# A recurrent attention block and its expert layer: the whole work order replaced by another

## The chip, the cores and the metric

The kernel runs on one core of a Trainium2 chip. The metric is device time in microseconds (us) of one execution; lower is better. The core has a matrix engine (PE in the profile, with its weight loads as PEld), three engines for elementwise work (DVE, ACT, POOL) and SP, which here only issues transfers. Each engine takes its instructions strictly in the order in which the program lists them; between engines only semaphores hold things together. So a list that says what comes after what on each engine decides when everything runs.

## The reference, cut to what matters

```python
for t in range(S):
    ...
    cur = np.einsum('bhd,bhe->bhde', u[None] * kt, vt)
    y[:, :, t] = np.einsum('bhd,bhde->bhe', rt, state + cur)
    state = w[None, :, :, None] * state + np.einsum('bhd,bhe->bhde', kt, vt)
...
pooled = x.mean(axis=1)
logits = pooled @ w_gate
e_idx = np.argmax(logits, axis=1)
...
    h = np.maximum(x[mask] @ w1[e], 0.0)
    out[mask] = gate_w[mask, None, None] * (h @ w2[e])
```

Batch is 4, heads 8, 768 steps, head width 48; x is the attention's output, (4, 768, 384), w1 is (8, 384, 1024), w2 (8, 1024, 384). A linear attention with a decaying state runs over four sequences of 768 steps; then each whole sequence is sent through one expert of eight, chosen from its mean.

## The kernel before, in words

Each sequence (batch b = 0 to 3) is cut into three blocks of 256 steps, so there are twelve blocks n = 0 to 11 with b = n / 3. The program is a set of small functions `do_X`, and a string of tokens, `ORDER`, which says in which order they are called. A token reads `what.arguments/engine@banks`: `E.5.1/V` calls `do_E` for block 5, half 1, on DVE; A is ACT, P is POOL; the digits behind @ are the PSUM banks (0 to 6) that its output takes. Tiles wait for each other by their data and by the reuse of a buffer or a bank; nothing else holds an engine. The scheduler does not move anything: an engine's queue is the string with the other engines' tokens taken out.

What the tokens do, along the path of a block:

- `L` loads k, r or v of a block (SP issues, L120); `cg` loads the gate's matrix (L263). `K` and `R` scale k and r by decay factors (POOL, L294; for block 0 in halves, `q`, `K.0`, `R.0`, L286). `V` casts v (tile vb).
- `T.n.0`, `T.n.1` turn scaled k and r on PE (tile tp, L325; from block 5 on L338). `E.n.0`, `E.n.1` copy the turned tiles out of PSUM (tile tw; L363 on DVE, L365 on ACT).
- `A` multiplies k with r on PE (tile at, L439), `G` masks the result on DVE (tile gt, L449): four per block, always DVE.
- `P`, `U`, `v`, `J` make the term of the current step: product on DVE or POOL, sum on PE (tile u, L399), times v (tile vt), and added on PE (L425). `t` copies a u tile out.
- `S` adds to the state on PE (L477, L468), `Z` decays it (DVE, L487), `s` copies it out (tile st), `y` multiplies r with it and `Y` the masked product with v, both on PE (tile y, L500).
- `N` casts the output out of PSUM (tile xn; L214 on DVE, L210 on ACT), `X` turns it on PE (tile xp, L538), `x` copies it to the expert's input xt; `p` and `g` sum it up.
- `l` is the gate's product on PE (tile lgp, L582, six matmuls), `m` takes the largest entry on DVE, `i` reads its number on POOL, `a` and `b` then load the chosen expert's first and second matrix (POOL issues, L627, L638). The transfer of the first matrix of batch 0 is split in two quarters, `a.0.q` and `a.0.0`, and a half, `a.0.1`.
- `M.b.f.s` is one group of the expert's first product (three matmuls into tile hp, L648; 64 tokens), `H` its ReLU (DVE or ACT, tile ht), `O.b.s.h` one group of the second (four matmuls into op, L683; 48 tokens), `o` the scaling by the gate, `B` the store (SP).
- `W.i.m` issues m matmuls of zeros into an otherwise unused bank (tile wp, L219); nothing reads them.

PE runs everything in one queue, so the groups `M` and `O` of one batch stand between the blocks of the next ones.

One thing ties loads to the expert's transfers: with `HOLD = (7, 8)` the loads of block 7 wait until the transfer `a.0.q` has landed, those of block 8 until the first `b` of a second half has (lines 267 to 276).

Of the kernel before, what the change touches and what calls it, by code (L numbers as in the profile page):

```python
# [24 lines left out]
v.0/P U.1@4 T.2.1@5 L.k.4 G.1.1.0/V Y.0@6 G.1.0.0/V y.1.0@1 y.1.1@0 s.2.0/A S.2.0 v.1/V Y.1 J.0 E.2.1/A
A.2.0@24 N.0.1/A N.0.0/A P.2/X K.3/P G.2.0.1/V G.2.0.0/V J.1 N.1.0/A N.1.1/A R.3/P L.r.4 L.v.4 A.2.1@53
G.2.1.0/V X.0@6 G.2.1.1/V V.3/A U.2@4 s.2.1/A T.3.0@1 p.0/V T.3.1@2 E.3.1/A X.1@0 E.3.0/V v.2/V p.1/V P.3/X
K.4/P y.2.1@5 S.3.0 s.3.1/A y.2.0@3 Y.2 J.2 N.2.0/A A.3.1@14 S.3.1 T.4.0@2 R.4/P x.1/A N.2.1/V Z.4/V G.3.1.0/V
X.2@3 E.4.0/A L.r.5 cg p.2/V g.0/V y.3.1@5 T.4.1@0 l.0@1 V.4/P G.3.1.1/V s.4.0/A m.0/V A.3.0@24 x.2/A x.0/A
E.4.1/A L.k.5 G.3.0.0/V G.3.0.1/V S.4.0 s.4.1/A W.2.4@1 U.3@3 v.3/V W.24.2@2 Y.3@6 e.0/A R.5/P L.r.6 A.4.0@14  # L30
A.4.1@23 P.4/X i.0/P S.4.1 a.0.q/P L.v.5 J.3 G.4.0.1/V G.4.1.0/V G.4.1.1/V G.4.0.0/V N.3.1/A N.3.0/A W.37.4@0
L.k.6 y.4.0@4 L.v.6 X.3@5 V.5/A U.4@0 K.5/P T.5.0@62 y.4.1@3 a.0.0/P T.5.1 Z.5/V p.3/A x.3/A Y.4 M.0.2.1@1
w.0/V E.5.0/V L.k.7 L.r.7 E.5.1/A s.5.0/A M.0.3.1@5 H.0.3.1/A H.0.2.1/A M.0.2.0@6 v.4/V H.0.2.0/V L.v.7 J.4
A.5.1@20 S.5.0 A.5.0@51 G.5.1.0/V a.0.1/P G.5.0.0/V M.0.0.1@6 K.6/P R.6/P P.5/P b.0.1/P N.4.1/A N.4.0/A
# [723 lines left out]
```

## Time and profile before

| | before |
|---|---|
| median of 3 runs | 129.71 us (129.59 to 130.69) |
| the profiled execution's own time | 129.35 us |
| its span, first to last instruction | 127.7 us |
| granted TensorE clock, mean | 0.999 of full speed |
| PE busy | 120.0 us (94%) |
| DVE, ACT, POOL busy | 84.7, 78.1, 78.0 us (66, 61, 61%) |
| moved by DMA | 25.5 MB |

The span leaves out what lies ahead of the first and behind the last instruction (1.6 us here). Busy shares are means over the span; the three elementwise engines do most of their work in the first 90 us, so a share read for a stretch says more than one of the whole. PE's matmuls overlap one another by their tails, so the duration of one (326 ns for a group's matmul of 384 columns) is longer than its share of PE's time (0.16 us, from a long row of them).

### The profile page before, as it was taken

What the parts mean: (1) busy time and instruction counts of PE and PEld (TensorE: products, weight loads), DVE (VectorE), ACT (ScalarE), POOL (GpSimd) and SP (SyncE); (2) the same over time, 40 slices, a digit from 0 to 9 for tenths busy, and PEclk for the clock granted to TensorE, in tenths of its full rate; (3) what the DMA queues carried; (4) which work ended last, traced back from release to release, by engine and by line L of the source; (5) the groups of instructions that cost most, each with busy time, mean ns of one, the idle gap of its engine ahead of it and who ended that gap; (6) DMA issues with size and microseconds to landing.
All of it is one profiled execution on the core that took longest, in us unless ns stands there. A gap on an engine that the chain in (4) does not pass through costs nothing.

```text
span 127.7 us, 4933 instructions
## 1 busy us (share of the span) xinstructions
PE 120.0 (94%) x2103; PEld 82.1 (64%) x2107; DVE 84.7 (66%) x192; ACT 78.1 (61%) x192; POOL 78.0 (61%) x72
## 2 busy tenths in 40 slices
...
GB/s 28 324 320 325 322 234 314 189 243 270 129 139 276 224 161 232 277 258 236 229 270 280 273 224 90 62 185 197 64 0 0 9 174 202 240 400 211 0 257 115
DMA packets 47768, 25.50 MB, mean 200 GB/s; under 512 B 38401, under 2 KB 46338, under 8 KB 47746
## 3 DMA queue, kind: packets, MB, share of 16 engines
...
## 4 chain that ended last, share of the span: by engine, by line
PE 91%; ACT 2%; DVE 2%; issue 2%; ACTq 0%
PE hp L648 25%; PE op L683 24%; PE y L500 8%; PE at L439 5%; PE wp L219 5%; PE tp L325 4%; PE tp L338 3%; PE xp L538 3%; PE s L468 3%; PE s L477 2%; PE lgp L582 2%; PE y L425 2%; PE u L399 2%; PE lnb L226 1%; PE op L673 1%
## 5 line engine op out<-in xcount | busy, mean ns | idle before, releaser
L648 PE MATMUL hp<-xt,w 128*128 128x384 bf16 x192 | 36.3, 326 | 0.0
L683 PE MATMUL op<-w,ht 128*128 128x384 bf16 x184 | 33.7, 326 | 0.0
L449 DVE TENSOR_TENSOR gt<-at,mask 128x512 bf16<-128x512 f32 x48 | 31.0, 683 | 3.8 <-PE at L439 3.5
L663 DVE TENSOR_SCALAR ht<-hp 128x384 bf16<-128x384 f32 x30 | 16.0, 552 | 13.3 <-PE hp L648 13.3
L683 PEld LDWEIGHTS <-ht 128*128 128x128 bf16 x184 | 17.4, 99 | 10.8 <-issue 0.2
L648 PEld LDWEIGHTS <-w 128*128 128x128 bf16 x192 | 17.4, 98 | 10.3 <-issue 0.3
L294 POOL TENSOR_TENSOR kp<-k,dk 128x768 bf16<-128x768 f32 x11 | 20.0, 1818 | 2.7 <-DMA k<-in_k_dram 2.1
L661 ACT ACTIVATE ht<-hp 128x384 bf16<-128x384 f32 x34 | 15.5, 501 | 9.4 <-PE hp L648 9.4
L294 POOL TENSOR_TENSOR rp<-r,dr 128x768 bf16<-128x768 f32 x11 | 20.0, 1814 | 1.6 <-DMA r<-in_r_dram 1.5
L704 ACT ACTIVATE ob<-op,gw 128x384 f32<-128x384 f32 (+1 forms) x17 | 9.5, 576 | 13.1 <-PE op L683 11.0
L627 POOL DMA_DIRECT2D w<-in_moe_w_dram x9 | 7.2, 797 | 15.7 <-issue 10.4
L365 ACT COPY tw<-tp 128x1024 bf16<-128x1024 bf16 x12 | 12.2, 1016 | 5.2 <-PE tp L338 4.6
L389 POOL TENSOR_TENSOR prod<-tw 128x1024 bf16<-128x1024 bf16 x6 | 12.7, 2121 | 1.8 <-DVE tw L363 1.8
L210 ACT CAST xn<-y 128x384 bf16<-128x384 f32 x22 | 9.7, 486 | 5.6 <-PE y L425 5.6
L706 DVE TENSOR_SCALAR ob<-op,gw 128x384 f32<-128x384 f32 (+1 forms) x8 | 4.6, 590 | 11.4 <-PE op L683 8.0
L495 ACT CAST st<-s 64x192 bf16<-64x192 f32 x32 | 10.1, 314 | 3.5 <-PE s L477 2.2
L219 PE MATMUL wp<-zeros 128*128 128x512 bf16 x30 | 9.0, 413 | 1.5 <-DVE zeros L135 1.4
L439 PE MATMUL at<-tw 64*64 64x128 bf16 x384 | 9.7, 219 | 0.4 <-DVE tw L363 0.2
L559 ACT ACTIVATE xt<-xp 128x256 bf16<-128x256 bf16 x21 | 7.8, 391 | 3.1 <-PE xp L538 3.1
L210 ACT CAST vb<-v 128x768 bf16<-128x768 f32 x10 | 8.4, 840 | 1.5 <-DMA v<-in_v_dram 1.5
L363 DVE COPY tw<-tp 128x512 uint32<-128x512 uint32 x12 | 8.1, 687 | 1.7 <-PE tp L338 0.8
L416 DVE TENSOR_TENSOR vt<-vb,u 128x768 bf16<-128x768 bf16 x8 | 7.6, 947 | 1.6 <-PE u L399 1.6
...
## 6 DMA issues: line engine op xcount, KB each, us to landing
w<-in_moe_w_dram POOLq DMA_DIRECT2D x15, 384.0 KB, 6.5
k<-in_k_dram SPq DMA_DIRECT2D x12, 384.0 KB, 5.2
r<-in_r_dram SPq DMA_DIRECT2D x12, 384.0 KB, 5.4
v<-in_v_dram SPq DMA_DIRECT2D x12, 384.0 KB, 5.9
out_dram<-ob SPq DMA_DIRECT2D x11, 384.0 KB, 6.9
w<-in_moe_w_dram POOLq DMA_DIRECT2D x2, 192.0 KB, 4.6
...
out_dram<-ob SPq DMA_DIRECT2D x1, 192.0 KB, 2.2
```

Source lines behind the costliest of these rows:

```text
L210: nc.scalar.copy(out, in_)
L219: nc.tensor.matmul(out=wp, lhsT=zeros[:, 0:128], rhs=zeros, start=True, stop=True)
L294: e.tensor_mul(dst[n % NR].rearrange("p (g a) d -> p a g d", a=2)[:, :, :, 0:D], *(t.rearrange("p (a q) j d -> p a (q j) d", a=2) for t in ...
L365: nc.scalar.copy(out, in_)
L389: e.tensor_mul(prod.rearrange("x g c p -> x c g p"), tk, tw[:, :, 1].rearrange("x c q j p -> x c (q j) p"))
L439: nc.tensor.matmul(out=at[a][64 * c : 64 * c + 64, 128 * q : 128 * q + 128], lhsT=tw[rows, c, 0, q, j, :], rhs=tw[rows, c, 1, q].rearrange ...
L449: nc.vector.tensor_mul(gts[n][:, j, a], ats[n, j][a].rearrange("x (q s) -> x q s", q=NQ), mask[:, j].rearrange("x j p -> x (j p)").unsquee ...
L500: nc.tensor.matmul(out=out, lhsT=lhsT, rhs=rhs, start=(n, c) not in begun, stop=False, skip_group_check=True)
L648: nc.tensor.matmul(out=hp[:, 0:SB], lhsT=wts[b][1][i][:, ct, 128 * f : 128 * f + 128], rhs=xts[b][:, ct, SB * sb : SB * sb + SB], start=(c ...
L661: nc.scalar.activation(out=o, in_=hp[:, 0:SB], func=ACT.Relu)
L663: nc.vector.tensor_scalar_max(o, hp[:, 0:SB], 0.0)
L683: nc.tensor.matmul(out=op[:, 0:DM], lhsT=hts[b, half][:, f, 128 * si : 128 * si + 128], rhs=wts[b][2][half][:, f, :], start=(half == 0 and ...
```

## The change

Only the string `ORDER` is replaced; every function, every buffer and every number of buffers stays. Both strings have 657 tokens and give PE the same 4168 rows of weight loads and matmuls. Apart from the labels of the filling matmuls and two small copies (`t.0` and `t.7` become `t.1` and `t.9`), the tokens are the same; they stand in another order, 72 have another engine, and nearly all PE tiles another bank.

```diff
-W.99.4@0 L.k.0 L.r.0 L.v.0 L.k.1 L.r.1 L.v.1 L.k.2 L.r.2 L.v.2 c.ln/A cB@0 c.dk.0/A c.dk.1/A W.33.2@1 W.15.2@2
...
+W.99.4@0 c.ln/A cB@0 c.dk.0/A c.dk.1/A c.dr.0/A c.dr.1/A L.k.0 q.k/P L.r.0 L.v.0 V.0/A L.k.1 W.37.2@1 W.2.4@2
...
```

The filling matmuls `W` number 34 in both; 14 stood ahead of the first `T` and 12 do now, and 10 stand behind `l.0` in both. On PE the same set of tokens stands ahead of the first `M` in both strings (fillers aside), in another sequence.

The first place is DVE's queue from its first copy out of PSUM on, that is blocks 0 and 1 (the digit behind a tile's letters is the block; for tp, gt and at further digits are halves). Before:

```order
L363 COPY tw0_221<-tp0_1_212 128x512
L363 COPY tw0_221<-tp0_0_227 128x512
L386 TENSOR_TENSOR prod0_251<-tp0_1_212,tw0_221 128x8x64 x2
L449 TENSOR_TENSOR gt0_290<-at0_01_255,mask_131 128x512
L449 TENSOR_TENSOR gt0_290<-at0_00_254,mask_131 128x512
L449 TENSOR_TENSOR gt0_290<-at0_10_272,mask_131 128x512
L487 TENSOR_TENSOR s0_237<-s0_237,wcT_168 128x384
L449 TENSOR_TENSOR gt0_290<-at0_11_273,mask_131 128x512
L363 COPY tw1_340<-tp1_1_342 128x512
L386 TENSOR_TENSOR prod1_375<-tp1_1_342,tw1_340 128x8x64 x2
```

DVE's queue at the same place, now:

```order
L363 COPY tw0_212<-tp0_1_214 128x512
L386 TENSOR_TENSOR prod0_240<-tp0_1_214,tw0_212 128x8x64 x2
L449 TENSOR_TENSOR gt0_286<-at0_11_244,mask_131 128x512
L449 TENSOR_TENSOR gt0_286<-at0_10_243,mask_131 128x512
L449 TENSOR_TENSOR gt0_286<-at0_00_261,mask_131 128x512
L487 TENSOR_TENSOR s0_223<-s0_223,wcT_168 128x384
L449 TENSOR_TENSOR gt0_286<-at0_01_262,mask_131 128x512
L416 TENSOR_TENSOR vt0_384<-vb0_182,u0_340 128x8x2x48
L386 TENSOR_TENSOR prod1_416<-tp1_1_312,tw1_337 128x8x64 x2
L449 TENSOR_TENSOR gt1_432<-at1_00_355,mask_131 128x512
```

Two of the three copies L363 have left the queue (`E.0.0` and `E.1.1`, now ACT's); the product with v of block 0 (L416) has come from POOL, which has that of block 1 instead. Up to the last `G` of block 4 one cast `N` goes (block 2) and one comes (block 3), one copy `p` goes and one copy `t` comes, and the rest of DVE's list is the same set.

The second place is DVE's queue behind the last `G` of block 5, with batch 0's `H` between the blocks. Before:

```order
L449 TENSOR_TENSOR gt5_1240<-at5_11_1189,mask_131 128x512
L663 TENSOR_SCALAR ht00_1172<-hp0_0_1_1245 128x384
L663 TENSOR_SCALAR ht00_1172<-hp0_1_0_1291 128x384
L363 COPY xt1_1117<-xp4_1261 128x2x3x64
L363 COPY tw6_1345<-tp6_0_1301 128x512
L416 TENSOR_TENSOR vt5_1371<-vb5_1062,u5_1347 128x8x2x48
L663 TENSOR_SCALAR ht10_1449<-hp0_6_0_1373 128x384
L214 CAST xn05_1455<-y5_0_1295 128x384
L449 TENSOR_TENSOR gt6_1467<-at6_10_1429,mask_131 128x512
```

The same place now:

```order
L449 TENSOR_TENSOR gt5_1282<-at5_00_1243,mask_131 128x512
L497 TENSOR_TENSOR st10_151<-s2_1308,bmask_155 128x384
L663 TENSOR_SCALAR ht10_1293<-hp0_6_1_1352 128x384
L363 COPY tw6_1407<-tp6_1_1318 128x512
L214 CAST xn05_1453<-y5_0_1357 128x384
L214 CAST xn15_1455<-y5_1_1367 128x384
L449 TENSOR_TENSOR gt6_1459<-at6_01_1416,mask_131 128x512
L363 COPY tw7_1496<-tp7_0_1462 128x512
L487 TENSOR_TENSOR s2_1308<-s2_1308,wcT_168 128x384
L363 COPY tw7_1496<-tp7_1_1463 128x512
```

Both casts of block 5 and both copies of block 7 are DVE's now. On PE, `Y.6`, which needs the four `G` of block 6, has moved up: behind the first `M` stood sixteen `M` and seven `O` ahead of it, now sixteen `M` and two `O`.

The third place is SP's queue, the loads of blocks 3 to 5. Before:

```order
L120 DMA v32_3_370<-in_v_dram 128x8x96
L120 DMA k32_4_465<-in_k_dram 128x8x96
L120 DMA r32_4_599<-in_r_dram 128x8x96
L120 DMA v32_4_601<-in_v_dram 128x8x96
L120 DMA r32_5_817<-in_r_dram 128x8x96
L263 DMA wg_108<-in_moe_w_gate_dram 128x3x8
L120 DMA k32_5_875<-in_k_dram 128x8x96
```

SP's queue at that place, now:

```order
L120 DMA v32_3_585<-in_v_dram 128x8x96
L263 DMA wg_108<-in_moe_w_gate_dram 128x3x8
L120 DMA k32_4_590<-in_k_dram 128x8x96
L120 DMA r32_4_685<-in_r_dram 128x8x96
L120 DMA v32_4_687<-in_v_dram 128x8x96
L120 DMA k32_5_786<-in_k_dram 128x8x96
L120 DMA r32_5_789<-in_r_dram 128x8x96
```

The gate's small load stands four loads earlier, ahead of k of block 4; the loads of blocks 0 to 3 have kept their sequence.

At the start, PE now turns k of block 0 first (`T.0.0`), then the small turn `cT` of w and u (L243, its input tile wu comes by two DMAs that POOL issues), then r (`T.0.1`); before it was `T.0.1`, `cT`, `T.0.0`. Between `S.0.0` and the first `A` stand four `W` matmuls in place of two.

## Rows read from the trace of the kernel before

**Rows 1.** The page, part 1: busy us, share of the span, instructions.

```profile
PE 120.0 (94%) x2103; PEld 82.1 (64%) x2107; DVE 84.7 (66%) x192; ACT 78.1 (61%) x192; POOL 78.0 (61%) x72
```

**Rows 2.** Windows: length; busy us (count) of PE, PEld, DVE, ACT, POOL; clock; DMA; GB/s.

```profile
8.14:36.00 27.86, 26.05 (x687) 20.74 (x692) 24.86 (x54) 20.75 (x44) 24.17 (x18) 1.00 1.02 254
36.00:54.00 18.00, 18.00 (x327) 12.43 (x326) 15.52 (x32) 11.84 (x28) 14.08 (x10) 1.00 1.06 221
36.00:124.20 88.20, 88.16 (x1402) 59.33 (x1400) 54.34 (x115) 52.30 (x142) 48.74 (x36) 1.00 0.84 184
```

**Rows 3.** Waits of PE, 8 to 36 us: us in total, times, longest.

```profile
PE s L468 <- issue: 0.7, 1, 0.7
PE xp L538 <- issue: 0.4, 1, 0.4
```

**Rows 4.** PE's groups, 8.14 to 36 us: busy us, mean ns, idle before.

```profile
L219 PE MATMUL wp<-zeros 128*128 128x512 bf16 x16 | 4.8, 381 | 0.2
```

**Rows 5.** Groups by form, whole span: busy us, mean ns, idle before, releasers.

```profile
L449 DVE TENSOR_TENSOR gt<-at,mask 128x512 bf16<-128x512 f32 x48 | 31.0, 683 | 3.8 <-PE at L439 3.5
L365 ACT COPY tw<-tp 128x1024 bf16<-128x1024 bf16 x12 | 12.2, 1016 | 5.2 <-PE tp L338 4.6 <-PE tp L325 0.5
L363 DVE COPY tw<-tp 128x512 uint32<-128x512 uint32 x12 | 8.1, 687 | 1.7 <-PE tp L338 0.8 <-PE tp L325 0.7
```

**Rows 6.** Timeline of DVE: start, us, what, idle before.

```profile
31.64 2.48 DVE L449 TENSOR_TENSOR gt<-at,mask 128x512 bf16<-128x512 f32 x4
35.66 0.69 DVE L363 COPY tw<-tp 128x512 uint32<-128x512 uint32 x1 [0.81 <-PE tp L338]
...
52.83 0.68 DVE L449 TENSOR_TENSOR gt<-at,mask 128x512 bf16<-128x512 f32 x1
```

**Rows 7.** Timeline of PE: block 0, T.4.1, the first gate, the first M, Y.6.

```profile
8.72 0.19 PE L243 MATMUL turned<-unit,wu 8*128 8x8 f32 x1
10.37 0.64 PE L439 MATMUL at<-tw 64*64 64x128 bf16 x32
...
26.82 0.61 PE L325 MATMUL tp<-unit,rp 128*128 128x128 bf16 x8
27.41 0.86 PE L582 MATMUL lgp<-wg,sums 128*128 128x8 f32 x6
...
35.96 1.64 PE L648 MATMUL hp<-xt,w 128*128 128x384 bf16 x9
...
56.37 0.56 PE L500 MATMUL y<-vb,gt 64*128 64x48 bf16 x32
```

**Rows 8.** Timeline of POOL, and DMA issues from 4 to 5.5 us (KB, us to landing).

```profile
4.79 0.61 POOL L200 DMA_DIRECT2D wu<-in_u_dram  x1
...
wu<-in_u_dram POOLq DMA_DIRECT2D x1, 1.5 KB, 3.8
```

**Rows 9.** Timeline of POOL, and its DMA issue: the first quarter of batch 0's w1.

```profile
30.50 0.81 POOL L627 DMA_DIRECT2D w<-in_moe_w_dram  x1 [2.81 <-DVE gt L449]
...
w<-in_moe_w_dram POOLq DMA_DIRECT2D x1, 192.0 KB, 4.5
```

**Rows 10.** Chain that ended last, 96 to 116 us; POOL and its issues for batch 3.

```profile
97.39 0.57 PE lgp L582 x6
...
100.09 7.15 PE op L683 x44
107.24 0.49 PE hp L648 x3
...
99.95 1.58 POOL L627 DMA_DIRECT2D w<-in_moe_w_dram  x2 [10.42 <-issue]
...
w<-in_moe_w_dram POOLq DMA_DIRECT2D x4, 384.0 KB, 7.1
```

**Rows 11.** SP's timeline (the gate's load), and POOL's (R.4).

```profile
20.64 2.37 SPq L263 DMA_DIRECT2D wg<-in_moe_w_gate_dram  x1
...
23.34 1.82 POOL L294 TENSOR_TENSOR rp<-r,dr 128x768 bf16<-128x768 f32 x1 [0.29 <-DMA r<-in_r_dram]
```

More of the change, by code (lines that the diff above doesn't have):

```diff
@@ L25 @@
[L25 to L34, printed above, removed]
@@ new lines @@
+K.0/V K.1/P q.r/V W.9.2@3 R.0/V T.0.0@4 cT@5 E.0.0/A T.0.1@6 S.0.0 W.24.4@1 L.r.1 E.0.1/V P.0/X A.0.1@02
+A.0.0@34 R.1/P ct/A L.v.1 s.0.1/A G.0.1.1/V G.0.1.0/V G.0.0.0/V y.0.1@5 T.1.0@1 S.0.1 T.1.1@6 W.29.2@2 cw/A
+Z.1/V V.1/A cu/P L.k.2 G.0.0.1/V L.r.2 E.1.0/A K.2/P U.0@0 E.1.1/A W.28.4@3 A.1.0@12 T.2.0@4 s.1.0/A v.0/V
+R.2/P W.5.2@3 S.1.0 A.1.1@03 P.1/X U.1@6 L.v.2 V.2/A G.1.0.0/V T.2.1@1 G.1.0.1/V E.2.0/A s.1.1/A Y.0@4 S.1.1
+E.2.1/A G.1.1.0/V t.1/V G.1.1.1/V J.0 N.0.0/A Z.2/V y.1.0@2 L.k.3 K.3/P T.3.0@0 P.2/X N.0.1/A s.2.0/A v.1/P
@@ new lines @@
+v.6/V T.8.1 Y.6@0 i.1/P S.7.0 a.1.0/P E.8.1/A A.7.1@53 o.0.5/V E.8.0/V J.6 P.7/P L.v.9 O.0.2.0@6 O.0.3.0@1
+s.7.1/A G.7.1.0/V V.8/P O.0.2.1 O.0.3.1 N.6.1/A S.7.1 N.6.0/A o.0.3/A G.7.1.1/V A.7.0@45 A.8.1@23 Z.8/V
+G.7.0.1/V G.8.1.1/V G.8.1.0/V O.0.4.0@0 P.8/P U.7@1 O.0.4.1 A.8.0@53 s.8.0/A o.0.2/V S.8.0 L.r.10 G.8.0.0/V
+G.7.0.0/V o.0.4/A V.9/A a.1.1/P U.8@2 R.9/P X.6@0 O.0.0.0@6 O.0.1.0@5 L.k.10 G.8.0.1/V O.0.0.1 M.1.2.0@4
+b.1.0/P K.9/P o.0.0/V s.8.1/A x.6/A M.1.3.0@3 M.1.1.0@0 H.1.3.0/A M.1.0.1@6 O.0.1.1 H.1.1.0/A v.7/V v.8/V
@@ new lines @@
+y.7.0@3 H.1.0.1/A o.0.1/A y.7.1@1 y.8.0@0 b.1.1/P H.1.2.0/V y.8.1@2 Y.7 T.9.0@64 Y.8 T.9.1 S.9.0 J.8 J.7
+E.9.0/V e.1/A s.9.1/A N.7.0/V K.10/P R.10/P E.9.1/V N.7.1/A M.1.4.0@5 M.1.3.1@6 N.8.1/V X.7@3 M.1.5.1@1
+M.1.6.0@4 N.8.0/V X.8@2 M.1.4.1@0 H.1.3.1/A H.1.4.0/A T.10.0@65 x.7/A x.8/A H.1.6.0/V H.1.4.1/V H.1.5.1/A
+B.0.2 L.r.11 R.11/P L.v.10 g.2/V L.k.11 S.9.1 A.9.0@43 G.9.0.1/V T.10.1 G.9.0.0/V M.1.7.1@0 l.2@2 M.1.2.1@1
+m.2/V w.1/V E.10.0/A V.10/A H.1.7.1/A Z.10/V s.10.0/V M.1.0.0@3 H.1.0.0/V M.1.1.1@6 H.1.2.1/V M.1.7.0@4 P.9/P
```

71 lines of the change are left out of this document (33 added, 38 removed).

## The prediction

> **What bounds the kernel now.** I read the page's busy shares first: PE is busy for 94% of the span [rows 1]. That share is a mean, so the windows come next. From 36.0 us, when the first expert group runs [rows 7], to 124.2 us PE is busy for 88.16 of 88.20 us [rows 2]: nothing waits there, and the change leaves PE's work as it is. Between 8.14 and 36.0 us PE is busy for 26.05 of 27.86 us [rows 2]. Sixteen recorded fillers are in that busy time [rows 4]; a matmul of 384 columns takes 7.15 / 44 = 0.163 us in a long row [rows 10], so one of 512 takes an estimated 0.22, and sixteen 3.5 us. So about 1.8 + 3.5 = 5.3 us ahead of the first `M` are not work, and nearly all that a new order can win lies there. With the same set of PE tokens ahead of the first `M` in both strings, three questions are left: when does the first `M` start, does PE stay full behind it, and does the end change?
>
> What holds PE ahead of 36 us is DVE: in that stretch DVE is busy for 24.86 of 27.86 us, ACT for only 20.75 [rows 2]. PE rarely waits by name, because fillers stand where DVE is late. Its two large gaps, 0.7 and 0.4 us, have "issue" as releaser [rows 3]: PE's sequencer had nothing ready, though PE waited for no other engine.
>
> **The start: 0.3 us later.** `cT` ran at 8.72 us [rows 7]. Its input was issued at 4.79 and took 3.8 us to land [rows 8], that is until 8.59 us; so it cannot run earlier, and in both orders one turn of block 0 and `S.0.0` stand between it and the first `A`, which ran at 10.37 us [rows 7]. Now four fillers stand there too in place of two: 2 x 0.22 = 0.4 us. The bounds are 0 (DVE, with one copy less, needs the time anyway) and 0.4; I take 0.3.
>
> **DVE's queue up to block 4: 1.25 us shorter.** Two copies of 687 ns leave it [rows 5]; the cast that goes and the one that comes have one shape and cancel, as do the two small copies: 1.37 us. Neighbours overlap, though: four `G` in a row take 2.48 us [rows 6], not 4 x 0.683 = 2.73 [rows 5]. The factor is 0.91, so 1.25 us. The copies go to ACT at 1016 ns each [rows 5]. With those, and with the casts and copies of blocks 2 and 3 that ACT now does ahead of that point, it has an estimated 4 us more to do; it was idle for 27.86 - 20.75 = 7.1 us [rows 2], so there is room, but less than before at the places where PE asks for `E.3.1`, `E.4.1` and `N.3.1`. If ACT is late there, the saving is 0, so the bounds are 0 and 1.25. I take the whole of it, because the last `G` of block 4 ended at 34.1 us [rows 6], 1.8 us ahead of the first `M`, and DVE was the fuller engine.
>
> The expert's weights set a floor under the first `M`. The gate's product began at 27.41 us [rows 7], the quarter's DMA started on POOL at 30.50 and landed 4.5 us later [rows 9]: 35.0 us, 0.96 ahead of its first use at 35.96 [rows 7]. With `m.0` earlier by up to 1.25 us the landing moves to 33.8, and POOL has one scaling between `V.4` and `i.0` in both orders. So the weights permit the saving.
>
> **Behind the first M: nothing, with a bound.** `Y.6` ran at 56.37 us, 20.4 us behind the first `M` [rows 7]. Five `O` that stood ahead of it now stand behind it, 5 x 4 x 0.163 = 3.25 us, and about 0.2 us of small groups: PE now gets there 17.0 us behind the first `M`. DVE has the same number of tokens as before between the last `G` of block 4 and the last of block 6, and of much the same kinds: 34.1 to 53.5 us [rows 6], 19.4 us, less the waits among them, 0.8 [rows 6] and 18.00 - 15.52 = 2.5 us [rows 2]: 16.1 us of work. It starts 0.9 to 1.8 us ahead of the first `M`, so it has 17.9 to 18.8 us for 16.1 plus its own waits; with the 3.3 us of waits that it had, it is at most 1.5 us late, without any it is 2.7 early. Stalls of PE: 0 to 1.5 us. I take 0, since much of the 3.3 us was idleness of an engine that was ahead.
>
> **The other batches' weights: 0.15 us.** The gate's product of batch 3 ended at 97.39 + 0.57 = 97.96 us, POOL issued at 99.95, and a transfer took a median of 7.1 us, so until about 107.0; the first `M` of batch 3 ran at 107.24 [rows 10]. The cover was three `M` and twelve `O`, 3 x 0.49 + 12 x 0.65 = 9.27 us; now it is three `M` and eleven `O`, 8.62, where 9.1 are needed. That is 0 to 0.5 us late; I take 0.15, as the first of four transfers in a row should land before the median.
>
> **The loads of block 4: nothing, with a bound.** The gate's small load held SP for 2.37 us, and r of block 4 already reached POOL 0.29 us late [rows 11]. It now stands ahead of k of block 4, so r may come up to 2.37 us later. POOL's scaling ended at 25.16 [rows 11] and PE used it at 26.82 [rows 7], so 1.66 us of that are covered: 0 to 0.7 us. I take 0.
>
> **The end.** The last PE group is the same half of block 11's last `O`, and the last store the same 96 KB: no change.
>
> **Sum.** On the profiled execution's own 129.35 us: 0.3 - 1.25 + 0.15 = -0.8, so 128.55. That execution lies 0.36 us under the median of the three runs; on the level of that median I predict **128.9 us**.
>
> **A rule and a row.** PE's gaps of 0.7 and 0.4 us lie where its sequencer had nothing ready [rows 3], in a stretch where the DMA engines are full (share 1.02 [rows 2]). My sum leaves these 1.1 us in, as both orders issue as many PE instructions there. The Trainium skill (Runtime: NRT & Kernel Launch, section Instruction fetch mechanics) says that an engine streams its instructions in blocks by its own DMA queue, and that the cost of crossing a block is mostly hidden. By that rule such gaps would not be there and the sum would be 1.1 us lower; the rows of before show them, so in this stretch the trace does not agree.
>
> **The rivals.**
> *The gaps go too.* If the sequencer now runs dry where PE stands in a wait or a filler anyway, the 1.1 us [rows 3] are hidden: 128.9 - 1.1 = 127.8 us. For it: the loads ahead of that point are nearly the same, so a gap stays, but it may fall under something else. Against it: with DVE's queue shorter there are fewer waits to hide under. Chance 0.22. The Trainium skill's rule above (Instruction fetch mechanics) would have it so.
> *DVE is late behind the first M.* This is the side on which it gets slower. Place: the last `G` of block 6 for `Y.6`, with the copy `E.6.1` for `A.6.0` on the way. Price: up to 1.5 us, with the 0.3 of the start and nothing won ahead of 36 us because ACT is then as tight as DVE was: 129.71 + 1.8 = 131.5 at most, 130.8 with half the stall. It decides from the point at which DVE ends that `G` more than 17.0 us behind the first `M`. Chance 0.22.
> *Nothing is won.* ACT's copies take the place of DVE's, the first `M` stands at 36 us as before and PE is full behind it: 129.7 us, 129.4 to 130.1. For it: ACT's copy takes half as long again as DVE's [rows 5]. Against it: ACT's 7.1 us of idleness. Chance 0.16.
>
> **How the numbers follow.** The forecast (first `M` 0.5 to 1.2 us earlier, PE full behind) has 0.40 and reaches from 128.3 to 129.4 us. What a measurement of this kernel can tell from no change is about 1%, 1.3 us: faster is below 128.4, slower above 131.0. Faster: the rival with the gaps (0.22) and the better edge of the forecast (0.08) make 0.30. Slower: the worse part of the DVE rival, 0.13. Within 1%: the other 0.57. The range of 127.7 to 130.8 leaves out the worse half of the DVE rival and the better edge of the gap rival, together under 0.2; the likeliest case's own range is 128.3 to 129.4.
>
> **What would show it.** Right: DVE's last `G` of block 4 ends near 32.9 us, the first `hp` matmul starts near 35.0 us, and PE is busy for the whole window behind it. The start is right if the first `at` matmul runs some 2.0 us behind `turned`, not 1.65. Gaps gone: no "issue" row of PE over 0.2 us. DVE late: waits of PE's `at` or `y` for DVE's `tw` or `gt` between 42 and 54 us. Weights: a wait of `hp` for `w` ahead of batch 3. The prediction is wrong in its ground if a load or a weight transfer stops PE for more than a microsecond, for then the order on SP and POOL, which I cost at nearly nothing, is what counts.

## The result, and the profile after

| | before | after |
|---|---|---|
| median of 22 runs each, on the same chip | 130.07 us (129.13 to 132.54) | 133.19 us (130.21 to 136.09) |
| the profiled execution's own time | 129.35 us | 133.07 us |
| its span | 127.7 us | 131.5 us |

The ratio of after to before is 1.0107, with a 95% interval from 1.0064 to 1.0149. That ratio leaves out 15 of the changed kernel's 22 executions, the profiled one among them, as more than 1.5% above its fastest; the medians lie 2.4% apart. Forecast were 128.9 us and a range up to 130.8: the sign was wrong, and the median lies 2.4 us outside the range.

The page's busy shares hardly differ from [rows 1]. Page of after, part 1 (busy us, share of the span, instructions):

```profile
PE 122.5 (93%) x2104; PEld 82.5 (63%) x2107; DVE 86.2 (66%) x197; ACT 76.8 (58%) x184; POOL 80.4 (61%) x75
```

The windows show where the time went. After, columns as in [rows 2] (length; busy us and count of PE, PEld, DVE, ACT, POOL; clock; DMA; GB/s):

```profile
8.14:36.00 27.86, 26.91 (x693) 20.57 (x697) 24.70 (x53) 23.31 (x46) 24.74 (x19) 1.00 1.08 262
36.00:54.00 18.00, 15.38 (x290) 10.49 (x292) 13.31 (x31) 9.41 (x26) 14.03 (x10) 0.91 1.11 243
47.70:51.10 3.40, 3.39 (x29) 2.13 (x30) 1.75 (x3) 1.03 (x6) 3.40 (x3) 0.50 0.94 243
54.00:100.00 46.00, 46.00 (x925) 31.61 (x926) 33.81 (x68) 27.72 (x79) 33.49 (x25) 1.00 0.76 148
```

Ahead of 36 us PE is busier than before (26.91 us, before 26.05). From 36 to 54 us, where it was full [rows 2], it is idle for 18.00 - 15.38 = 2.62 us, and for 3.4 us in the same stretch the granted clock is 0.50, its lower level of 1.2 GHz. From 54 to 100 us it is full again. The waits of PE in after (us in total, times, longest), to be read beside [rows 3]:

```profile
PE tp L338 <- POOL rp L294: 1.6, 1, 1.6
PE wp L219 <- DVE zeros L135: 1.4, 1, 1.4
PE s L468 <- issue: 0.8, 1, 0.8
PE turned L243 <- DMA wu<-in_u_dram: 0.7, 1, 0.7
PE y L500 <- issue: 0.3, 1, 0.3
```

Three idle times are new behind the first `M`: the turn of r of block 7 (`T.7.1`) waits 1.55 us for POOL's scaling of it (`R.7`), and PE stands twice, for 0.81 and 0.26 us, with "issue" as releaser. No wait is for DVE's `tw` or `gt`. Timeline of PE in after: the small turn, the first `at`, the first `M` (beside [rows 7]), three idle times and the end.

```profile
8.84 0.19 PE L243 MATMUL turned<-unit,wu 8*128 8x8 f32 x1 [0.75 <-DMA wu<-in_u_dram]
10.93 0.64 PE L439 MATMUL at<-tw 64*64 64x128 bf16 x32
...
34.50 1.15 PE L648 MATMUL hp<-xt,w 128*128 128x384 bf16 x6
...
38.37 0.34 PE L468 MATMUL s<-vb,kp 64*64 64x48 bf16 x11 [0.81 <-issue]
...
47.71 0.61 PE L338 MATMUL tp<-ident,rp 64*128 64x64 bf16 x16 [1.55 <-POOL rp L294]
...
126.12 1.48 PE L673 MATMUL op<-w,ht 128*128 128x192 bf16 x16
```

The first `M` runs at 34.50 us, 1.46 earlier than in [rows 7]. PE ends at 127.60, 3.45 later than before (124.15). In this one pair of traces: -1.46 at the first `M`; +2.62 idle; +1.70, an estimate, for 3.40 us at half the clock; and 0.59 us more that PE shows as busy (see "What stays open"). Behind PE's end 0.3 us more follow: 3.8 us, the difference of the spans.

What `R.7` waited for is on POOL. Timeline of POOL in after (L627 and L638 issue the expert's transfers, L294 scales):

```profile
33.31 0.81 POOL L638 DMA_DIRECT2D w<-in_moe_w_dram  x1
34.14 1.82 POOL L294 TENSOR_TENSOR kp<-k,dk 128x768 bf16<-128x768 f32 x1
35.90 0.80 POOL L627 DMA_DIRECT2D w<-in_moe_w_dram  x1
...
37.47 0.78 POOL L638 DMA_DIRECT2D w<-in_moe_w_dram  x1
38.27 1.83 POOL L294 TENSOR_TENSOR rp<-r,dr 128x768 bf16<-128x768 f32 x1
40.96 1.80 POOL L294 TENSOR_TENSOR kp<-k,dk 128x768 bf16<-128x768 f32 x1 [0.86 <-PE hp L648]
45.85 1.80 POOL L294 TENSOR_TENSOR rp<-r,dr 128x768 bf16<-128x768 f32 x1 [3.09 <-DMA r<-in_r_dram]
```

The two `b` transfers of batch 0 are issued at 33.31 and 37.47 us. Before, this is where they stood, behind `P.5`:

```profile
40.32 1.56 POOL L638 DMA_DIRECT2D w<-in_moe_w_dram  x2
42.42 1.81 POOL L294 TENSOR_TENSOR kp<-k,dk 128x768 bf16<-128x768 f32 x1 [0.55 <-PE tp L338]
...
46.29 1.80 POOL L294 TENSOR_TENSOR rp<-r,dr 128x768 bf16<-128x768 f32 x1
```

So in after five expert transfers (a.0.q and a.0.1 at 29.93 us, then b.0.1, a.0.0, b.0.0) surround the loads of block 7, which `HOLD` releases as a.0.q lands. The chain of work that ended last, in after, goes through them (start, us, what):

```profile
29.93 4.27 DMA w<-in_moe_w_dram
...
34.71 11.01 DMA r<-in_r_dram
...
45.86 1.81 POOL rp L294
...
47.71 0.61 PE tp L338 x15
```

A load of 384 KB took 11.01 us to land, where the median over the loads of r was 5.4 us before and 5.8 after. That comparison is too hard on it, since the three loads of block 7 are issued within 1.3 us of one another in both orders. The trace of before has no landing for r of block 7; k, issued just ahead of it, landed at 42.26 us and v, just behind it, at 44.70. If the three landed in their order, r took 6.7 to 9.2 us there.

### The profile page after: what moved, and what is told of

Its sections match the earlier page's. It is cut to its first block, busy times and chain, and to the rows that moved or that the text cites. A ratio compares the mean times of both kernels' runs of the same rounds, so it can differ in the third digit from the quotient of the medians.

```text
span 131.5 us, 4936 instructions
## 1 busy us (share of the span) xinstructions
PE 122.5 (93%) x2104; PEld 82.5 (63%) x2107; DVE 86.2 (66%) x197; ACT 76.8 (58%) x184; POOL 80.4 (61%) x75
## 4 chain that ended last, share of the span: by engine, by line
PE 76%; DMA 15%; DVE 2%; POOL 1%; issue 1%; POOLq 1%; ACT 0%; SPq 0%; DVEq 0%
PE op L683 23%; PE hp L648 21%; DMA r<-in_r_dram 8%; PE y L500 5%; PE at L439 4%; PE wp L219 3%; DMA w<-in_moe_w_dram 3%; PE xp L538 3%; DMA wu<-in_u_dram 3%; PE tp L325 3%; PE tp L338 2%; PE s L477 2%; PE u L399 2%; PE y L425 2%; PE s L468 2%; POOL rp L294 1%
## 5 line engine op out<-in xcount | busy, mean ns | idle before, releaser
L648 PE MATMUL hp<-xt,w 128*128 128x384 bf16 x192 | 37.4, 333 | 0.0
L648 PEld LDWEIGHTS <-w 128*128 128x128 bf16 x192 | 18.0, 100 | 11.5 <-issue 1.7
L294 POOL TENSOR_TENSOR rp<-r,dr 128x768 bf16<-128x768 f32 x11 | 20.0, 1820 | 6.0 <-DMA r<-in_r_dram 5.9
L661 ACT ACTIVATE ht<-hp 128x384 bf16<-128x384 f32 x34 | 15.7, 494 | 11.4 <-PE hp L648 11.2
L294 POOL TENSOR_TENSOR kp<-k,dk 128x768 bf16<-128x768 f32 x11 | 20.0, 1819 | 3.5 <-DMA k<-in_k_dram 1.8
L365 ACT COPY tw<-tp 128x1024 bf16<-128x1024 bf16 x14 | 14.1, 1013 | 5.3 <-PE tp L338 4.4
L704 ACT ACTIVATE ob<-op,gw 128x384 f32<-128x384 f32 (+1 forms) x16 | 8.9, 561 | 12.3 <-PE op L683 9.8
L627 POOL DMA_DIRECT2D w<-in_moe_w_dram x9 | 7.1, 793 | 11.6 <-DVE ob L706 6.7
L219 PE MATMUL wp<-zeros 128*128 128x512 bf16 x31 | 10.2, 448 | 1.4 <-DVE zeros L135 1.4
L363 DVE COPY tw<-tp 128x512 uint32<-128x512 uint32 x10 | 6.9, 687 | 5.4 <-PE tp L338 3.9
L706 DVE TENSOR_SCALAR ob<-op,gw 128x384 f32<-128x384 f32 x9 | 5.5, 614 | 7.1 <-PE op L683 7.1
L210 ACT CAST xn<-y 128x384 bf16<-128x384 f32 x17 | 7.6, 480 | 3.1 <-PE y L425 2.8
L416 POOL TENSOR_TENSOR vt<-vb,tcol 128x768 bf16<-128x768 bf16 x4 | 6.0, 1509 | 3.8 <-ACT tcol L210 3.7
L439 PEld LDWEIGHTS <-tw 64*64 64x64 bf16 x384 | 6.8, 106 | 1.8 <-issue 0.5
```

What stands on the lines that cost most here:

```text
L219: nc.tensor.matmul(out=wp, lhsT=zeros[:, 0:128], rhs=zeros, start=True, stop=True)
L294: e.tensor_mul(dst[n % NR].rearrange("p (g a) d -> p a g d", a=2)[:, :, :, 0:D], *(t.rearrange("p (a q) j d -> p a (q j) d", a=2) for t in ...
L365: nc.scalar.copy(out, in_)
L439: nc.tensor.matmul(out=at[a][64 * c : 64 * c + 64, 128 * q : 128 * q + 128], lhsT=tw[rows, c, 0, q, j, :], rhs=tw[rows, c, 1, q].rearrange ...
L648: nc.tensor.matmul(out=hp[:, 0:SB], lhsT=wts[b][1][i][:, ct, 128 * f : 128 * f + 128], rhs=xts[b][:, ct, SB * sb : SB * sb + SB], start=(c ...
L661: nc.scalar.activation(out=o, in_=hp[:, 0:SB], func=ACT.Relu)
```

## The experiments

Theory L: the early `b` transfers and the held loads of block 7 share the DMA engines, so r (or k) of block 7 lands late, PE stops for it, and the clock falls. Rivals: PE asks for block 7 too early (its turns moved up); DVE is late behind the first `M`; the front gains less than it seems. All edits are edits of the string; in runs whose string was written anew the line numbers are 3 lower (L645 for L648, L291 for L294). "Kernel before" in the table is its median in the same session; where no ratio stands, the record has none.

| run | median us (range, runs) | kernel before | ratio, 95% | first M us |
|---|---|---|---|---|
| e0: after again | 134.19 (132.82 to 135.93, 4) | 130.84 | 1.029 (1.016 to 1.042) | 34.76 |
| e1: both b later | 131.80 (129.57 to 132.94, 4) | 129.91 | | 35.47 |
| e1h: e1, block 8 not held | 131.33 (129.63 to 132.86, 10) | 129.91 | 1.005 (0.999 to 1.010) | 34.78 |
| e10: b.0.1 alone later | 133.46 (133.16 to 134.25, 4) | 129.69 | 1.030 (1.025 to 1.035) | 34.75 |
| e8: block 7 not held | 131.66 (131.23 to 132.14, 4) | 129.98 | 1.017 (1.009 to 1.024) | 35.74 |
| e2: turns of block 7 later | 132.95 (132.28 to 133.75, 4) | 129.91 | 1.024 (1.016 to 1.031) | 34.69 |
| e3: fillers ahead of T.7.1 | 133.09 (131.80 to 134.56, 4) | 129.91 | 1.030 (1.022 to 1.038) | 34.42 |
| e5: before, both b early | 132.95 (130.26 to 134.60, 4) | 129.98 | | 37.72 |
| e5r: the same again | 133.80 (129.74 to 135.47, 4) | 129.69 | | 35.78 |
| e4: before, all four early | 134.71 (133.70 to 136.98, 4) | 130.84 | 1.033 (1.018 to 1.047) | 35.45 |
| h1: after's front, before's rest | 131.50 (131.36 to 132.29, 4) | 130.84 | 1.014 (1.004 to 1.024) | 34.63 |
| h2: before's front, after's rest | 134.62 (132.74 to 136.24, 4) | 130.84 | 1.026 (1.011 to 1.041) | 35.45 |
| e11: two copies back on DVE | 132.46 (131.72 to 135.63, 4) | 129.69 | 1.019 (1.015 to 1.023) | 35.85 |
| e6: before, two copies on ACT | 134.88 (131.64 to 136.01, 4) | 129.98 | | 38.95 |
| e7: e1h, small turn later | 131.77 (130.74 to 133.05, 6) | 129.98 | 1.012 (1.004 to 1.020) | 35.71 |

### Is the wait for block 7 there every time? (e0)

The string unchanged.

> The changed kernel unchanged, for a second trace. Theory L (its loads of block 7 share the DMA engines with four expert transfers): the scaling of r of block 7 on POOL waits 2 to 3 us for its load again, PE stands 1 to 2 us for it, and the time is 130.5 to 135 us. If the wait of the first trace was a matter of that one execution, the wait is gone and the time is 129 to 130.5 us.

PE's wait is larger than expected. Timelines of e0, POOL and PE:

```profile
44.44 1.80 POOL L291 TENSOR_TENSOR kp<-k,dk 128x768 bf16<-128x768 f32 x1 [4.12 <-DMA k<-in_k_dram]
48.38 1.80 POOL L291 TENSOR_TENSOR rp<-r,dr 128x768 bf16<-128x768 f32 x1 [2.14 <-DMA r<-in_r_dram]
...
50.24 0.61 PE L335 MATMUL tp<-ident,rp 64*128 64x64 bf16 x16 [3.53 <-POOL rp L291]
```

Here k of block 7 is late too, PE stops for 3.53 us, and the granted clock over 36 to 54 us is 0.81. A third trace, of e11 below, has the same order but for the engine of two copies; there the stop is short and the clock stays at 1.00:

```profile
48.41 0.41 PE L335 MATMUL tp<-ident,rp 64*128 64x64 bf16 x16 [0.63 <-POOL rp L291]
```

The wait is in all three traces; its size changes from execution to execution (1.55, 3.53, 0.63 us), and the time goes with it (133.07, 135.93, 132.46 us).

### Taking the transfers or the load out of each other's way (e1, e1h, e10, e8)

e1 moves both `b`; e1h has `HOLD = (7, 99)` on top, so that the loads of block 8 don't wait for the moved `b.0.1`.

```diff
-T.5.0@01 b.0.1/P Y.4
+T.5.0@01 Y.4
...
-V.6/P b.0.0/P G.5.1.0/V
+V.6/P G.5.1.0/V
...
-R.6/P H.0.6.0/V
+R.6/P b.0.1/P b.0.0/P H.0.6.0/V
```

> The new order with the two transfers of batch 0's second matrix (b.0.1, b.0.0) moved on POOL behind R.6, where the old order had them. Theory L (the load of r of block 7 shares the DMA engines with expert transfers that now stand ahead of it): r of block 7 lands near 41.5 us in place of 45.7, T.7.1's wait of 1.55 us goes, PE's clock stays at its upper level, and the time falls by the wait, the 1.7 us of the half clock and part of the gaps: 128 to 129.5 us on the level of 129.7 for the kernel before. A risk by the same theory: loads of block 8 stand back until b.0.1 has landed, so T.8.0 may wait then. Rival P (T.7 has moved up too far on PE, whatever the transfers do): r lands little earlier, a wait of over 1 us stays at T.7.1. Rival D (DVE late behind the first M): no change, 131 us or more.

> As the run with the two transfers moved behind R.6, and the loads of block 8 no longer wait for a transfer of the second matrix (the second number of HOLD is out of reach). Theory L: T.7.1 does not wait, nor does T.8.0; 127.5 to 129 us. If the first of the two runs shows a wait at T.8.0 and this one does not, that wait came from the loads' standing back. Rival P: a wait of over 1 us at T.7.1 stays. Rival D: no change.

Timeline of POOL in e1:

```profile
38.84 1.55 POOL L635 DMA_DIRECT2D w<-in_moe_w_dram  x2
41.49 1.81 POOL L291 TENSOR_TENSOR kp<-k,dk 128x768 bf16<-128x768 f32 x1 [1.10 <-DMA k<-in_k_dram]
43.27 1.81 POOL L291 TENSOR_TENSOR rp<-r,dr 128x768 bf16<-128x768 f32 x1
```

`R.7` waits for nothing: r was there at most 7.4 us after its issue at 35.91, where it took 11.01 in after. PE doesn't wait for block 7, and in this trace the clock stays up. The medians are 1.9 and 1.4 us over the kernel before of the same session, where after's and e0's are 3.1 and 3.4 over it; e1h's ratio can't be told from 1 (1.005, with 1 in the interval). Two points were missed: the times were not under the kernel before, so about half of the loss stays, and e1's first `M` came later (35.47).

e10 moves `b.0.1` alone, to behind `R.6`.

```diff
-T.5.0@01 b.0.1/P Y.4
+T.5.0@01 Y.4
...
-R.6/P H.0.6.0/V
+R.6/P b.0.1/P H.0.6.0/V
```

> The changed kernel with b.0.1 alone moved back behind R.6; b.0.0 stays where it is, and the loads of block 8 still wait for b.0.1. Theory L: with one of the transfers out of the way, the wait of POOL for r of block 7 (3.1 us) shrinks to 0 to 1.5 us, PE waits for it at most 0.3 us, and the time lies between the changed kernel and the run with both moved: 131 to 132.5 us. If the number of transfers doesn't matter: 133 us with the wait of 1 us and more on PE.

POOL's wait for r of block 7 is 2.25 us and PE's 0.77, both smaller, as theory L has it, but not as small as expected (at most 1.5 and 0.3). The time did not fall into the expected range: block 8's loads, held until `b.0.1` has landed, came late in their turn. Timeline of PE in e10:

```profile
52.72 0.41 PE L335 MATMUL tp<-ident,kp 64*128 64x64 bf16 x16 [2.18 <-POOL kp L291]
```

e8 leaves the transfers and lets the loads go.

```diff
-    HOLD = (7, 8)
+    HOLD = (99, 8)
```

> The changed kernel without the rule that the loads of block 7 wait until the first quarter of the expert's weights has landed. Theory L, as far as it says the load of r comes late because it starts only at 34.7 us and then shares with four transfers: r of block 7 lands before 40 us, no wait of POOL or PE for it, and the clock does not fall. The quarter of the weights shares with the loads instead and lands later, so the first M moves from 34.5 to 35 to 36.5 us: 130 to 132 us in all. If PE stands for block 7 all the same, the load is not its cause: 132 to 135 us.

The trace and the median are as theory L expected. The first `M` and the windows of e8:

```profile
35.74 1.15 PE L648 MATMUL hp<-xt,w 128*128 128x384 bf16 x6 [0.54 <-DMA w<-in_moe_w_dram]
```

```profile
36.00:54.00 18.00, 17.50 (x380) 12.10 (x378) 15.70 (x36) 9.82 (x28) 15.27 (x13) 1.00 1.17 253
54.00:100.00 46.00, 45.45 (x866) 31.19 (x859) 32.92 (x68) 28.30 (x83) 32.57 (x23) 1.00 0.75 140
```

No wait for block 7, clock at 1.00 in this execution, and the price is at the front, where the first `M` now waits for its weights. So moving the transfers and moving the loads both take the stop away: the late load is the cause of the stop. That it is late because of the early transfers is shown by e1, where only the transfers moved, and by e5r below. e8 alone would not show it, since there the loads also start 5.6 us sooner (k of block 7 at 28.66 us, in after at 34.25).

The mean granted clock of every execution is on record too. It was below 0.99 in 15 of the 26 executions of the changed order (after and e0), in 7 of the 24 of e1, e1h, e8 and e7 (which is e1h with one more move, see below), and in 5 of the 37 of the kernel before in the same sessions. So such executions are fewer without the late load, but not as few as in the kernel before; what PE stood for in those seven, none of them traced, is open.

### PE asks too early, or the clock alone? (e2, e3)

e2 moves the turns of block 7 and their copies behind six more groups `M`; e3 puts seven matmuls of zeros (`W.50.7@0`) ahead of `T.7.1`, so that PE has something to do while it waits.

```diff
-T.7.0@16 T.7.1 E.7.0/V Z.7/V
+Z.7/V
...
-M.0.1.0@1 E.7.1/V x.5/A
+M.0.1.0@1 x.5/A
...
-H.0.5.0/V w.0/V
+H.0.5.0/V T.7.0@04 T.7.1 E.7.0/V E.7.1/V w.0/V
```

> The new order with T.7.0, T.7.1 and their copies E.7.0, E.7.1 moved later, behind the last M of batch 0's first product (3.9 us of PE work later; banks 0 and 4 in place of 1 and 6, since those are free there). The transfers stay. Rival P, and theory L too (whatever makes r late, PE has other work until it is there): no wait at T.7.1, clock at its upper level; 128 to 130 us, less some tenths for T.8.0 and A.6.1 that now wait for two copies on DVE. If r's lateness were not what stops PE, the time would stay at 131 to 133 us. Rival D: the same, and DVE's copies would now be waited for longer.

```diff
-T.7.0@16 T.7.1
+T.7.0@16 W.50.7@0 T.7.1
```

> The new order with seven filling matmuls (1.5 us) between T.7.0 and T.7.1, so that PE does work that nobody reads where it waited. It adds work and takes none away. If the fall of the clock behind the wait is a loss of its own (theory C): the wait of 1.55 us stays as fillers, but the clock stays at its upper level, and the time falls by about 1.7 us against the new order where that had the fall: 130.5 to 131.5 us with little scatter. If the clock does not matter: no change, or up to 1.5 us slower when r lands early.

In e2 POOL still waits 0.89 and 1.78 us for k and r of block 7. PE no longer stops there, but the turns of block 8 come right behind those of block 7 and wait for its copies, and the clock falls behind that wait, for 3.4 us from 53.37. Timeline of PE in e2:

```profile
51.64 0.41 PE L335 MATMUL tp<-ident,kp 64*128 64x64 bf16 x16 [1.38 <-DVE tw L360]
```

The edit made a wait of its own, and the time (132.95, expected 128 to 130) missed its range. So e2 tells little on the place of the turns, except that moving the consumer doesn't bring the load any sooner, and the rival that PE asks too early is answered by e1 and e8 alone. e3 kept PE at work and the clock at 1.00 from 36 to 54 us (the trace has six of the seven fillers):

```profile
46.01 1.68 PE L216 MATMUL wp<-zeros 128*128 128x512 bf16 x6
47.63 0.41 PE L335 MATMUL tp<-ident,rp 64*128 64x64 bf16 x16
```

PE ended at 126.19 us in this execution, the fastest of four, 1.41 before that of after, near the 1.70 that the half clock is worth. But the mean clock was 1.000 in all four, and their median (133.09, expected 130.5 to 131.5) is that of after. So the loss does not need the fall of the clock; how it divides in the three executions without a trace is not shown.

### The transfers early in the order of before (e5, e5r, e4)

e5 and e5r are one kernel: before, with both `b` right behind `a.0.1`.

```diff
-a.0.1/P G.5.0.0/V
+a.0.1/P b.0.1/P b.0.0/P G.5.0.0/V
...
-P.5/P b.0.1/P N.4.1/A
+P.5/P N.4.1/A
...
-E.6.1/A b.0.0/P K.7/P
+E.6.1/A K.7/P
```

> The kernel before with only b.0.1 and b.0.0 moved, from behind P.5 and behind E.6.1 to right behind a.0.1 on POOL, so that all of batch 0's expert transfers are under way with the loads of block 7, as in the changed kernel; no other transfer changes place. Theory L (transfers and loads share the DMA engines): r of block 7 lands at 44 to 46 us in place of 42. PE turns block 7 only at 49.9 us in this order and POOL scales r from 46.3, so if the changed kernel's loss needs both the early transfers and the earlier turns of block 7, the time is 129.7 to 131 us. If the early transfers alone bring the loss: 131.5 us or more, with a wait of PE in the stretch from 36 to 54 us.

> The kernel before with b.0.1 and b.0.0 right behind a.0.1, once more, for a trace without a gap ahead of the moved transfers. Theory L: the load of k of block 7, issued near 35 us, lands at 44 us or later in place of 42, POOL waits for it, and the time is again 1 to 3 us over before's: 131 to 133 us. If the first run of this kernel was slow through its early gap alone: 129.7 to 130.5 us.

3.0 and 4.1 us over the kernel before by the medians: the early transfers alone bring a loss, although PE turns block 7 late in this order. They don't bring it every time: one execution of four ran in 130.26 us in e5 and in 129.74 in e5r, like the kernel before. e5's trace has a gap of 1.56 us ahead of the moved transfers; e5r's is cleaner. There k of block 7 took 10.5 us to land (7.2 before), and this is what came of it, on POOL and on PE:

```profile
44.94 1.81 POOL L291 TENSOR_TENSOR kp<-k,dk 128x768 bf16<-128x768 f32 x1 [3.52 <-PE at L436]
46.71 2.12 POOL L386 TENSOR_TENSOR prod<-tw 128x1024 bf16<-128x1024 bf16 x1
...
48.88 0.35 PE L396 MATMUL u<-U,prod 128*128 128x8 bf16 x8 [1.72 <-POOL prod L386]
```

`K.7` is 2.5 us later than before (42.42). POOL's releaser is given as PE's `at`, but that had long been done: 34.29, the issue of k, and 10.5 give 44.8, so it is the load. Behind `K.7` in POOL's queue stands the product of block 6, and PE waits for that. My theory had looked for the wait at the turns of block 7 and allowed "just cover" there; the cover was used up by what was queued behind the load, not by the load's own consumer.

e4 moves all four transfers and puts `a.0.1` and `b.0.1` ahead of `a.0.0`, as the changed order does.

```diff
-a.0.q/P L.v.5
+a.0.q/P a.0.1/P L.v.5
...
-K.5/P T.5.0@62 y.4.1@3 a.0.0/P T.5.1
+K.5/P b.0.1/P a.0.0/P T.5.0@62 y.4.1@3 T.5.1
...
-a.0.1/P G.5.0.0/V M.0.0.1@6 K.6/P R.6/P P.5/P b.0.1/P N.4.1/A
+G.5.0.0/V M.0.0.1@6 K.6/P b.0.0/P R.6/P P.5/P N.4.1/A
...
-E.6.1/A b.0.0/P K.7/P
+E.6.1/A K.7/P
```

> The kernel before with its four expert transfers of batch 0 issued as early as in the changed kernel (a.0.1 behind the quarter, b.0.1 and a.0.0 behind K.5, b.0.0 behind K.6), nothing else. Theory L by itself: r of block 7 lands some 4 us later (45 to 46 us in place of 42); PE turns block 7 at 49.9 us here and POOL scales r from 46.3, so there is just cover for it: 129.7 to 130.5 us, with a wait of POOL for r of block 7. If PE stands for it all the same: 131 to 133 us, and the transfers' place alone is the loss. If r lands no later than 43 us the sharing is not the cause.

This one failed as a test. The groups `M` of before need the quarter `a.0.0` as third, my edit put two halves ahead of it, and PE stopped for that (timeline of PE in e4):

```profile
41.32 1.14 PE L645 MATMUL hp<-xt,w 128*128 128x384 bf16 x3 [2.98 <-DMA w<-in_moe_w_dram]
```

### The two halves of the order (h1, h2)

h1 takes the changed order up to the first `M` (without `a.0.1`, `b.0.1` and `L.k.7`, which stay where before has them) and then before's; h2 the reverse. Twelve PSUM banks (three in h2) behind the seam were chosen anew where the old one was still in use.

```diff
-W.99.4@0 L.k.0 L.r.0 L.v.0 L.k.1 L.r.1 L.v.1
...
-T.5.1 Z.5/V p.3/A x.3/A Y.4 M.0.2.1@1 w.0/V
+W.99.4@0 c.ln/A cB@0 c.dk.0/A c.dk.1/A c.dr.0/A c.dr.1/A
...
+Y.4 T.5.1 V.5/A e.0/A a.0.0/P Z.5/V M.0.2.1@5 w.0/V
```

> The changed order up to the first M (with the two transfers a.0.1 and b.0.1 and the load of k of block 7 left where the kernel before has them), then the order of before for all that is left; some PSUM banks at the seam are chosen anew. If the time won ahead of the first M is real and the loss lies wholly behind it: first M near 34.5 to 35.0 us as in the changed kernel, PE full behind it for the 88.2 us of before, so 1.0 to 1.4 us under before: 128.5 to 129.0 us on before's 129.9. If the gain ahead of the first M is only fillers and work shifted, or if before's order behind it leans on the later start: 129.7 to 131 us.

> The other half: the order of before up to the first M, then the changed order for all that is left. If the loss lies behind the first M: PE takes there 1.5 to 4 us more than the 88.2 us of before, 131.5 to 134 us. If the loss comes from how the two halves of the changed order fit (its early start meeting loads that are held), a later start gives the loads time and it is 129.7 to 130.5 us.

h1's first `M` runs at 34.63, and nothing is won: its time (131.50) is above both of the expected ranges. PE waits from 36 us on for vt and gt (0.21 and 0.40 us), then for a `H` that ACT does late (timeline of PE in h1):

```profile
47.35 1.62 PE L645 MATMUL hp<-xt,w 128*128 128x384 bf16 x9 [1.67 <-ACT ht L658]
```

So the order of before behind the first `M` leans on the start that it had: with PE 1.3 us earlier and DVE's last `G` of block 4 only 0.57 us earlier (31.07 + 2.48 = 33.55), DVE and ACT have become the late ones. How much of it the new banks caused I can't say. h2 stops for r of block 7 again, by 2.29 us, although its start is before's: the stop comes from the order from the early transfers on, not from the earlier start. Its time (134.62) is above the expected range; PE also waits 0.95 and 0.73 us for ACT and DVE near the seam, which after does not have.

### The front (e11, e6, e7)

e11 undoes the two copies that the prediction's main term rests on; e6 does them alone in the order of before.

```diff
-E.0.0/A
+E.0.0/V
...
-E.1.1/A
+E.1.1/V
```

> The changed kernel with the copies E.0.0 and E.1.1 back on DVE, all else in its order. By the prediction's main term DVE's queue to block 4 is 1.25 us longer again: the first M moves from 34.5 to 35.2 to 35.8 us, and since the loads of block 7 then start as much later, the time is 133 to 134.5 us. If the earlier start comes from other moves of the order (the small turn, the fillers, N and x): first M at 34.4 to 34.9 us, time 132.5 to 133.5 us.

> The kernel before with one part of the change alone: the copies E.0.0 and E.1.1 go to ACT. The prediction's main term: DVE's queue to block 4 gets 1.25 us shorter, the first M comes 0.5 to 1.2 us earlier (34.8 to 35.5 us), and 128.7 to 129.5 us on before's 129.9. If these copies are not what holds PE (ACT's copy takes 1.0 us where DVE's takes 0.7, right at the start where each block waits for its copies): first M at 35.9 us or later, 129.7 to 130.5 us.

Timelines of e11, DVE and PE:

```profile
31.20 2.47 DVE L446 TENSOR_TENSOR gt<-at,mask 128x512 bf16<-128x512 f32 x4
...
32.98 0.22 PE L535 MATMUL xp<-unit,xn 128*128 128x128 bf16 x1 [1.01 <-issue]
...
35.85 1.15 PE L645 MATMUL hp<-xt,w 128*128 128x384 bf16 x6
```

The first `M` does come 1.35 us later than in after, as expected, but not for DVE: its last `G` of block 4 ends at 33.67 us, where it ended at 33.42 in after and, with the copies on ACT, at the same 33.67 in e0. PE has an issue gap of 1.01 us that the traces of after and e0 do not have; less the gap, the first `M` is about as early as e0's (34.76). The time of e11 (132.46) lies at the lower edge of the second expected range, that of e6 (134.88) over both of its ranges. In e6 the second copy stands behind others in ACT's queue, and PE waits for it (timeline of PE in e6):

```profile
17.67 0.76 PE L436 MATMUL at<-tw 64*64 64x128 bf16 x32 [2.58 <-ACT tw L362]
```

At the last `G` of block 4, moving the copies is worth 0 to 0.25 us with the rest of the changed order around it. Without it, it costs PE a stop of 2.6 us in this trace, whose first `M` is 3.0 us later than before's.

e7 moves the small turn.

```diff
-T.0.0@4 cT@5 E.0.0/A T.0.1@6 S.0.0
+T.0.0@4 E.0.0/A T.0.1@6 cT@5 S.0.0
```

> Of the run with the two b transfers moved back and the loads of block 8 not held (e1h), with the small turn cT moved behind the second turn of block 0, where the kernel before has it. By the prediction's step on the start, PE no longer stands 0.5 to 0.9 us for its input at 8 us: the first at 0.2 to 0.6 us earlier, and 0.2 to 0.6 us less in all, 130.2 to 131.0 us beside e1h's 131.3, near before's. If the fillers behind it or DVE take the time up, no change: 131.3 us.

The first `at` comes 0.57 us earlier than in e1h (10.80), but the first `M` 0.93 us later: PE waits 0.72 us for one of ACT's copies, and there is an issue gap of 0.46 us at 32.84. Timeline of PE in e7:

```profile
10.23 0.64 PE L436 MATMUL at<-tw 64*64 64x128 bf16 x32
...
17.84 0.57 PE L497 MATMUL y<-vb,gt 64*128 64x48 bf16 x32 [0.72 <-ACT tw L362]
...
35.71 1.15 PE L645 MATMUL hp<-xt,w 128*128 128x384 bf16 x6
```

No version ran faster than the kernel before.

## Why the prediction was wrong, step by step

**The bound.** That "nothing waits there" was right of [rows 2], but I read from it that the stretch behind the first `M` would look after itself. That it was full in one order says nothing of another.

**The start, +0.3.** Right in kind, 0.56 us in size (first `at` at 10.93, before 10.37, and 2.09 us behind `turned`). Whether it costs anything at the first `M` is not shown: e7 took it away, and the first `M` came later, behind a wait and a gap that e1h does not have.

**DVE's queue, -1.25.** This step gave the expected sign by the wrong means. I forecast the last `G` of block 4 at 32.9 and the first `M` near 35.0 us; they came at 33.42 and 34.50. DVE's part is 34.12 - 33.42 = 0.70 us, of which e11 leaves at most 0.25 to the copies. The other 0.76 us is about the size of the issue gap of 0.7 us at 32.48 [rows 3], which the trace of after does not have; from that `G`'s end to the first `M` it took 1.84 us before, 1.08 in after, 1.09 in e0 and, with a gap of 1.01, 2.18 in e11. So the mis-sized term is this one: I took the whole of a queue's shortening (bounds 0 and 1.25), although DVE was idle for 3.0 us in that stretch [rows 2], where a copy less may only lengthen a wait.

**The weights.** Forecast to land at 33.8 us, they landed at 34.20 (29.93 + 4.27), 0.3 ahead of the first `M`: they permit 34.50 and hardly less. e8 shows the floor: with loads beside it the transfer was late and PE waited 0.54 us for it.

**Behind the first M, 0.** This is the step that failed. I asked only whether DVE would be late, and it was not: no wait of PE for `tw` or `gt`. What came was a load. The change puts `b.0.1` and `b.0.0` 7.0 and 3.6 us earlier on POOL (33.31 and 37.47, before 40.32 and 41.1) while `HOLD` releases block 7's loads, and I gave neither a cost. In the traces of the changed order that brought a stop of 1.55 us with 3.4 us at half the clock, and one of 3.53 with 6.8. The last sentence of the prediction named this possibility as the one that would break its ground, "for then the order on SP and POOL, which I cost at nearly nothing, is what counts"; it had no place among the rivals and no chance. It should have had one: [rows 9, 10] show transfers that take 4.5 and 7.1 us to land, and the order of POOL's queue was there to be read. The step also took the matmuls behind the first `M` to cost the same in any order, with no gap among them: in e8, without the late load, PE still takes 1.0 us more there in issue gaps and 0.7 us more while busy.

**Batch 3's weights, +0.15.** No wait of PE for them in after: zero. **The loads of block 4, 0:** right; POOL scaled r of block 4 at 23.77 us without a wait. **The end, 0:** 0.3 us too little. From PE's end to the span's it is 3.85 us, before 3.58, and 3.8 to 4.1 in every trace with the changed order behind the first `M`, 3.6 in every other. The two last stores now stand right behind each other on SP, and the last one is issued 0.74 us behind PE's end (128.34 us), before 0.49 (124.64).

**The rivals.** *The gaps go too* was half right: no issue gap ahead of 36 us in after, but 0.81 and 0.26 us behind. In these traces the gaps moved; they didn't go. *DVE is late* came nearest in time (130.8 to 131.5), on the right side, by a mechanism that did not happen in the changed kernel; in h1, with the same early start and before's order behind it, PE waits 0.61 us for DVE and, longer, 1.67 us for ACT. *Nothing is won* fits the ratio of e1h (1.005), the changed order without the late load, but not by its mechanism: the first `M` there is 1.2 us earlier.

**What stays open.** With the late load out of the way, the early first `M` still wins nothing. Behind it PE takes 88.20 us in the kernel before. In e8 it takes 89.93 us with 1.05 idle, in e1 90.12 with 1.30, in e1h 92.63 with 3.28: without the idle time 88.9, 88.8 and 89.4. So 0.6 to 1.2 us are spent in stretches that the trace shows as busy, for the same matmuls. Part of it can be placed: counted from each matmul's start to the next one's (idle times over 0.15 us left out), the groups `s` and `y` take 9.95 us in the kernel before and 10.7 to 11.2 in all eleven traces with the changed order behind the first `M`; with before's order they take 9.9 to 10.2 in the other runs, though 10.7 in e6. In e8 and e1 the attention's other groups on PE give back 0.4 and 0.6 us of it. Why these groups take longer in the new sequence no run tests. And of the executions of the changed order whose mean clock was above 0.99 (10 of the 22, 130.21 to 133.69 us) none was traced; the nearest trace is e11's, with a stop of 0.63 us for block 7 and 2.35 us of issue gaps.
